# An attention block and a gated MLP in one kernel on one Trainium2 core: a fixed order of scores, maxima and dense products, and weights split by GpSimd

## The chip, the cores and the metric

The kernel runs on one core of a Trainium2 chip, all in float32. The metric is the device time of one execution in microseconds. Three timed runs of the kernel before took 1990.43, 1990.27 and 1982.49 us; the median is 1990.27 us. The profile is of another execution, which took 1979.48 us; its span, from the first to the last instruction, is 1977.7 us.

Five engines work side by side, each through its own queue in order: TensorE (PE: matmuls into PSUM, with weight loads of its own, PEld), VectorE (DVE), ScalarE (ACT), GpSimd (POOL) and SyncE (SP, which here issues nearly all transfers).

## The reference

`x` is 2048 x 512. The result is `x + A(xn) + B(xn)`, where `xn` is the layer norm of `x`:

```python
def _A_ref(x, wqkv, wo):                       # H = 32 heads of 16
    qkv = transpose((x @ wqkv).reshape(B, S, 3, H, Dh), 2, 0, 3, 1, 4)
    q, k, v = qkv[0], qkv[1], qkv[2]
    scores = jnp.einsum("bhqd,bhkd->bhqk", q, k) * (Dh ** -0.5)
    p = _softmax(scores, axis=-1)
    o = jnp.einsum("bhqk,bhkd->bhqd", p, v)
    return transpose(o, 0, 2, 1, 3).reshape(B, S, D) @ wo

def _B_ref(x, w_in, w_sp, b_sp, w_out):        # Fh = 896
    z = _gelu(jnp.einsum("bsd,df->bsf", x, w_in))
    z1 = z[..., :Fh]
    z2 = _layernorm(z[..., Fh:], axis=-1)
    g = jnp.einsum("ts,bsf->btf", w_sp, z2) + b_sp[None, :, None]
    return jnp.einsum("bsf,fd->bsd", z1 * g, w_out)
```

## The kernel before, in words

**Precision.** Nearly all matmul operands are float32r pairs: a value is split into a high part (a copy rounded to float32r) and a low part (the value minus its high part). A product is three matmuls, high x high, low x high and high x low. A weight comes from memory as a raw float32 tile, and `weight()` makes its two parts: the high one on ScalarE or on GpSimd, whichever has less planned work at that point, the low one on GpSimd.

**Attention.** There are 16 pairs of heads, 4 groups of 512 queries and 16 tiles of 128 keys, so 1024 score tiles. For each, `scores()` issues two matmuls (one for each head of the pair, in the two halves of TensorE's rows) into one of three PSUM tiles `sl`, and ScalarE writes their exponential into a tile `pf` (line 63). A softmax needs the row's maximum first: `maxima()` issues the transposed score tile, again two matmuls into one of the three `sl`, and VectorE reduces it (line 754). After every 16 maxima `max_fin` turns the maxima into two extra rows of the operand `qst` by way of memory (`mscr`), so that the scores come out with the maximum taken off. `values()` closes a cycle of CYC = 8 score tiles: it multiplies eight `pf` with `vall`, 32 matmuls that add up in one of the three `sl`. 1024 / 8 = 128 cycles. Every fourth pair `norm_out` fetches sums from memory, divides and stores the attention output as high and low parts (`ohl`).

**Dense work.** Beside the attention run all other products, one after the other, as generators in a list `queue`: Q and K of the other heads (`qk_rest`), the second half of `w_in` (`z2_all`), its first half (`z1_all`), the spatial product (`spatial`: four groups of 512 columns, each with 16 tiles `wsp` of weights against tiles `zs` of the normed z2, in seven units; the last unit of a group is "lone"), the MLP's output (`mlp_out`) and the attention's output (`attn_out`). A dense slot is two matmuls in the two halves of the rows, into the two banks of `dps`. GELU, layer norm, splits and stores of this work, called side work here, are generators too; each step names its engine (`"A"` ScalarE, `"D"` VectorE, `"G"` GpSimd, `"T"` a time that only passes, `"C"` a condition).

**The order.** The whole program is written out by a planner at build time, in Python. It holds an estimated time for TensorE (`T["P"]`) and for the other engines, and the loop at the end of `fused_block` chooses the next TensorE slot: a score or a maximum whenever one of three `sl` is free and a bound allows it, chosen by the backlog of ScalarE and VectorE; else a dense slot; else, after 0.7 us of planned idle time, a filler (two matmuls into `dps` whose result isn't used, line 1103). When eight scores are out and their exponentials planned, it issues `values()`. `advance` places side work on an engine as soon as the plan has the engine free. The engines' queues then hold that order for good: an instruction whose input is late holds up all that stand behind it on its engine.

**Memory.** One ring, `big`, has RING = 18 pieces of 4 KB a partition: weights, `zs`, `xnT`, operands of the outputs. A counter, `room`, says how many are free in the plan. Raw weights have a ring of their own of three half pieces (tag `raw`). `load_z` is called for the tile two places ahead when a quarter of a unit is done. Nearly all loads and stores are issued by SP (`move`, line 115), in the order of the plan: a load whose buffer is still in use holds up all later ones.

Two lines carry the old choice and the old high part:

```python
min(pick, key=lambda p: p[0])[1]()                        # a score or a maximum, by backlog
if max(T["A"], clock()) < max(T["G"], clock()): ...       # weight(): high part by ScalarE or GpSimd
```

Of the kernel before, what the change touches and what calls it, by code (L numbers as in the profile page):

```python
# [31 lines left out]
RING = 18  # L32
LEAD = 24
PF = 7
# [11 lines left out]
def fused_block(ctx, tc, x, wqkv, wo, w_in, w_spT, b_sp, w_out, out):  # L46
# [51 lines left out]
    oscr = [dr.tile([P, 2, S], F32, name=f"oscr{g}") for g in range(4)]  # L98
# [47 lines left out]

    room = {"hilo": 3, "ogrp": 1, "raw": 3, "big": RING}

# [74 lines left out]
    def begin(nm, src, n, blocks=1, t=None, early=None):  # L223


        t = piece(nm) if t is None else t
        rw = t512(nm + "r") if early == "t" else big.tile([P, 512], F32, tag="raw", name=nm + "r", bufs=3)
        dst, hi = rw[:, :n], t[:, 0, :n]
        if blocks > 1:
            src = src.rearrange("(c p) f -> p c f", p=P)  # L230
            dst, hi = (v.rearrange("p (c f) -> p c f", c=blocks) for v in (dst, hi))
# [3 lines left out]
        return t, rw, n  # L235

    def end(loaded, early=False):
        t, rw, n = loaded
        if early:
            nc.vector.tensor_sub(t[:, 1, :n], rw[:, :n], t[:, 0, :n].bitcast(F32))  # L240
        else:
            gps(0.6).tensor_copy(t[:, 0, :n], rw[:, :n])
            gps(1.3).tensor_sub(t[:, 1, :n], rw[:, :n], t[:, 0, :n].bitcast(F32))
        return t

    def prepare(out, loads, freed=None, spare=0):
        for k, *a in loads:
            spawn(weight(out, k, a, freed, spare), 2)

    def weight(out, k, a, freed, spare):  # L250
        yield "C", lambda: room["raw"] > 0 and room["big"] > spare and (freed is None or freed and freed[0] <= clock())
        lease("raw", -1)
        if freed:
            freed.pop(0)
        t, rw, n = begin(*a)
        yield "T", LOAD
        if max(T["A"], clock()) < max(T["G"], clock()):
            yield "A", ta(n)
            act(t[:, 0, :n], rw[:, :n], AF.Copy)
        else:  # L260
            yield "G", 0.61
            nc.gpsimd.tensor_copy(t[:, 0, :n], rw[:, :n])
        yield "G", 0.0026 * n
        nc.gpsimd.tensor_sub(t[:, 1, :n], rw[:, :n], t[:, 0, :n].bitcast(F32))
        lease("raw", 1)
# [137 lines left out]
    def qk_rest():  # L403
        for g in range(NG):
            for m in range(1, 4):
                if m == 3 and g + 1 < NG:
                    fetch_xnT(g + 1, 1)
# [4 lines left out]
                if g == NG - 1 and m == 1:  # L412
                    prepare(w2, [((c, j), f"w2_{c}_{j}", w_in[c * P:(c + 1) * P, FH + j * 448: FH + (j + 1) * 448], 448) for c in range(ND) for j in range(2)], spare=2)
# [27 lines left out]
    def z2_norm(t, z):  # L441

        u = piece(f"z2u{t}").bitcast(F32).rearrange("p a b -> p (a b)")[:, :FH]
# [13 lines left out]
        st = sm.tile([P, 2, 6], F32, tag="zst", name=f"zst{t}", bufs=2)  # L457
        mv = sm.tile([P, 2], F32, tag="zmv", name=f"zmv{t}", bufs=2)
        rs = sm.tile([P, 3], F32, tag="zrs", name=f"zrs{t}", bufs=2)
# [37 lines left out]
    def z2_all():  # L497
        yield from need(lambda: len(w2) == 2 * ND)
        for t in range(NT):
            xt = xts.pop(t)  # L500
            if t + 2 < NT:
                z2_load(t + 2)
            if t == NT - 3:
                prepare(w1, [(f, f"w1_{f}", w_in[:, f * P:(f + 1) * P], D, ND) for f in range(NF)], spare=3)
            if t == NT - 1:
                fetch_xnT(0, 0.5)
            z = piece(f"z2_{t}").bitcast(F32).rearrange("p a b -> p (a b)")[:, :FH]
# [24 lines left out]
    def z1_gelu(f, g, bank, x, u):  # L532
# [13 lines left out]
        after(2.5, lease, "big" if bank else "hilo", 1)  # L546

    def z1_all():
        for g in range(NG):
# [3 lines left out]
            for n, pair in enumerate(pairs):  # L553
                if g == NG - 1 and n == 2:
                    load_b(0)
                    load_z(0)
                    load_z(1)
                    prepare(wsp, [((0, s), *sp_weights(0, s)) for s in range(NT)])
                if n == (2 if g % 2 else 1) and g + 1 < NG:
                    fetch_xnT(g + 1, 1)  # L560
# [28 lines left out]

    def load_z1(g, f):  # L590
# [7 lines left out]
    def spatial():  # L598
        ahead = RING - NT
        for n, (g, (x, y)) in enumerate(units):  # L600
# [7 lines left out]
            freed = []  # L608
            if lone:
                if g + 1 < NG:  # L610
                    prepare(wsp, [((g + 1, s), *sp_weights(g + 1, s)) for s in range(NT)], freed)
                else:
                    prepare(wout, [(f, f"wout{f}", w_out[f * P:(f + 1) * P, :], 512) for f in range(NF)], freed)
# [3 lines left out]
            for s in range(NT):  # L617
                yield from need(lambda: (g, s) in wsp)
# [6 lines left out]
                if lone:  # L625
                    freed.append(clock() + HALF)
                    lease("big", 1)
                    if g + 1 == NG and s == NT - 4:
                        mlp_load(0, 0)
                if s % 4 == 3:  # L630
                    lease("big", 1)
                    if 4 * n + s // 4 + ahead < len(zparts):
                        later(0.7, load_z, 4 * n + s // 4 + ahead)
# [61 lines left out]
    def mlp_out():  # L695
# [13 lines left out]
        for t in range(0, NT, 2):  # L709
            xt = load_x(t)  # L710
            if t == NT - 4:
                selectors()
                prepare(wo_, [(g, f"wo{g}", wo[g * P:(g + 1) * P, :], 512) for g in range(4)])
# [66 lines left out]
    def norm_out(g4, c):  # L780
# [6 lines left out]
        both_ = at_.tile([P, 3, 512], F32, tag="ogrp", name=f"ob{g4}_{c}", bufs=1)  # L787
# [10 lines left out]
        after(5.0, move, both_[rows, 2, :], rscr[g4][c][:nh].rearrange("h (o x) -> h o x", o=1).to_broadcast([nh, DH, 512]))  # L798
# [431 lines left out]
```

## Time and profile before

| | us or share |
|---|---|
| timed runs, median (lowest, highest) | 1990.27 (1982.49, 1990.43) |
| profiled execution: time, span | 1979.48, 1977.7 |
| mean granted TensorE clock | 0.968 |
| GpSimd, VectorE, ScalarE busy, share of the span | 32%, 73%, 64% |
| transfers | 293.55 MB, 148 GB/s |

In the lines that follow, a group or an instruction is given as line of the program, engine, operation, output <- inputs, shapes and count. In a view of stretches each row has the stretch in us from the span's start, its length, the busy time of the engines shown with the number of their instructions, the granted TensorE clock (1.00 is full speed), the share of the DMA engines' time and GB/s. In a view in order of time the first number is the start, the second the duration; brackets hold the engine's idle time just before and what ended it. SPq is SyncE's queue as it issues a transfer. In a list of waits the numbers are the total in us, how often, and the longest.

### The profile page before, as it was taken

Reading aid. Unit: us, or ns where it says so; the run is one execution under the profiler, and the core shown is the slowest. Engines: PE = TensorE matmul, PEld = TensorE weight load, DVE = VectorE, ACT = ScalarE, POOL = GpSimd, SP = SyncE. Lnnn points to the kernel's source line nnn. Section 1 sums busy time; section 2 is a strip of 40 time slices with the busy share of each in tenths; the row PEclk is TensorE's granted clock in tenths of the full one; section 3 lists DMA queues with packets and bytes.
Section 4 is the critical chain, followed back from the end, with each engine's and each line's share of the span. In section 5 each row is a group of like instructions: output and inputs, shape, how many; then the busy total and the mean of one; then the engine's idle time right before and its main releaser. Section 6 shows DMA issues by size and latency. Waiting matters only on the chain. (4 is left out here: it accounts for less than half of the span.)

```text
span 1977.7 us, 37714 instructions
## 1 busy us (share of the span) xinstructions
PE 1866.4 (94%) x14506; PEld 1113.1 (56%) x14506; DVE 1445.2 (73%) x1677; ACT 1257.5 (64%) x1401; POOL 625.5 (32%) x693
## 2 busy tenths in 40 slices
PE   7989999999999999999999899989999999999897
PEld 6755665565565656555655565655655555434552
DVE  5377878888787767776876677757778888767772
ACT  4337778788777756666655566656666666655554
POOL 3222358878988830051014300230023001001100
PEclk9999999999999999999999999999999999878898
DMA  9564653546544554656568564564658755411321
GB/s 325 187 203 162 231 137 103 144 116 156 174 141 149 148 145 120 152 174 146 149 159 214 139 151 126 164 148 129 151 167 197 182 136 150 128 28 56 104 84 64
DMA packets 236588, 293.55 MB, mean 148 GB/s; under 512 B 37352, under 2 KB 137384, under 8 KB 233528
## 3 DMA queue, kind: packets, MB, share of 16 engines
q1 hardware_dynamic: 232184, 281.10, 51.9%
q0 software_dynamic: 4224, 10.04, 1.4%
q8 instruction: 114, 1.87, 0.4%
q14 instruction: 66, 0.54, 0.1%
HBM read 189.08 MB, written 101.98 MB: 147 GB/s over the span
## 5 line engine op out<-in xcount | busy, mean ns | idle before, releaser
L754 DVE TENSOR_REDUCE mm<-sl 128x2 f32<-128x1024 f32 x1024 | 1218.6, 1223 | 273.3 <-PE sl L1046 256.4
L63 ACT ACTIVATE pf<-sl 128x1024 f32<-128x1024 f32 x1024 | 1043.5, 1026 | 488.3 <-PE sl L1032 295.6
L1126 PE MATMUL sl<-pf,vall 128*32 128x512 f32 x4096 | 486.8, 615 | 12.8 <-DVE mm L754 6.0
L1032 PE MATMUL sl<-qst,kst 50*128 50x512 f32 x2048 | 448.8, 425 | 23.0 <-DVE mm L754 12.0
L1046 PE MATMUL sl<-kst,qst 48*128 48x512 f32 x2048 | 447.2, 423 | 21.3 <-ACT pf L63 14.2
L1090 PE MATMUL dps<-wsp,zs 64*128 64x512 f32 x2688 | 441.4, 400 | 20.6 <-DMA zs<-z2scr 18.0
L1090 PEld LDWEIGHTS dps<-wsp,zs 64*128 64x128 f32 x2688 | 276.5, 190 | 74.9 <-DMA zs<-z2scr 24.4
L1032 PEld LDWEIGHTS sl<-qst,kst 50*128 50x128 f32 x2048 | 205.3, 189 | 188.2 <-DVE mm L754 79.5
L1046 PEld LDWEIGHTS sl<-kst,qst 48*128 48x128 f32 x2048 | 202.4, 188 | 174.3 <-ACT pf L63 76.7
L1126 PEld LDWEIGHTS sl<-pf,vall 128*32 128x32 f32 x4096 | 124.8, 112 | 302.4 <-issue 252.8
L1146 DVE TENSOR_TENSOR e<-sl,e 128x512 f32<-128x512 f32 x64 | 44.3, 692 | 167.2 <-PE sl L1126 153.7
L666 POOL TENSOR_TENSOR hhl<-z1i,hhl 128x512 fp32r<-128x512 f32 x28 | 35.6, 1287 | 404.4 <-ACT hhl L63 404.4
L1090 PE MATMUL dps<-w,xt 64*128 64x448 f32 x768 | 111.1, 369 | 1.5
L1090 PE MATMUL dps<-wout,hp 64*128 64x512 f32 x672 | 105.4, 393 | 0.0
L800 POOL TENSOR_TENSOR ob<-ob 128x512 f32<-128x512 f32 (+1 forms) x16 | 20.6, 1285 | 249.8 <-DMA ob<-escr 249.8
L63 ACT ACTIVATE e<-sl 128x512 f32<-128x512 f32 x64 | 38.2, 597 | 75.2 <-PE sl L1126 70.0
L1090 PEld LDWEIGHTS dps<-w,xt 64*128 64x128 f32 x768 | 73.5, 186 | 16.3 <-issue 8.0
L1090 PEld LDWEIGHTS dps<-wout,hp 64*128 64x128 f32 x672 | 64.3, 187 | 10.0
L803 POOL TENSOR_TENSOR ob<-ob 128x512 f32<-128x512 f32 (+1 forms) x16 | 20.6, 1286 | 138.8 <-DMA ob<-rscr 138.8
L399 POOL TENSOR_TENSOR qkhl<-qr,qkhl 128x512 fp32r<-128x512 f32 x24 | 30.5, 1286 | 105.3 <-ACT qkhl L63 105.3
L1090 PE MATMUL dps<-wo,op 64*128 64x512 f32 x288 | 50.8, 429 | 0.9
L484 POOL TENSOR_TENSOR z2hl<-z,z2hl 128x512 fp32r<-128x512 f32 (+1 forms) x32 | 36.8, 1150 | 2.2
(297 smaller groups left out, 1554.0 us busy)
## 6 DMA issues: line engine op xcount, KB each, us to landing
zs<-z2scr SPq DMA_DIRECT2D x192, 256.0 KB
escr<-e SPq DMA_DIRECT2D x60, 256.0 KB
hscr<-hhl SPq DMA_DIRECT2D x28, 512.0 KB
qst<-qscr SPq DMA_DIRECT2D x30, 384.0 KB
kst<-kscr SPq DMA_DIRECT2D x30, 384.0 KB
xscr<-xnT POOLq DMA_DIRECT2D x16, 512.0 KB, 6.1
qscr<-qkhl SPq DMA_DIRECT2D x16, 512.0 KB
kscr<-qkhl SPq DMA_DIRECT2D x16, 512.0 KB
```

What stands on the lines that cost most here:

```text
L63: return nc.scalar.activation(out, in_, func, **kw)
L399: nc.gpsimd.tensor_sub(hl[:, 1, :], raw_, hl[:, 0, :].bitcast(F32))
L484: nc.gpsimd.tensor_sub(hl[:, 1, :w], z[:, lo:lo + w], hl[:, 0, :w].bitcast(F32))
L666: nc.gpsimd.tensor_sub(hl[:, 1, :], z1, hl[:, 0, :].bitcast(F32))
L754: nc.vector.tensor_reduce(mmax[g][:, :, t, kc], sl[k], AX.X, ALU.max)
L800: nc.gpsimd.tensor_add(both_[rows, 0, :], both_[rows, 0, :], both_[rows, 1, :])
L803: nc.gpsimd.tensor_mul(both_[rows, 0, :], both_[rows, 0, :], both_[rows, 2, :])
L1032: nc.tensor.matmul(sl[k][:, j, :], kst[p % 2][rows, kt * P:(kt + 1) * P], qst[p % 2][rows, c * 512:(c + 1) * 512], start=True, stop=True)
L1046: nc.tensor.matmul(sl[k][:, j, :], qst[p % 2][rows, tt * P:(tt + 1) * P], kst[p % 2][rows, kc * 512:(kc + 1) * 512], start=True, stop=True)
L1090: nc.tensor.matmul(dps[:, bank, :w], lhs, rhs, start=go, stop=stop)
L1126: nc.tensor.matmul(sl[k][cols:cols + VW, 0, :], vpack(kt + r, 2 * p + j), pf[:, j * 512:(j + 1) * 512], start=n == n_pv, stop=n == n_pv + ...
L1146: nc.vector.tensor_add(e, sl[k][:, 0, :], e)
```

## The change

Four things change together.

1. The order. A cycle pair has a fixed order, written as two strings of S (scores), M (maxima), D (dense) and V (values). The loop goes through them letter by letter. A letter whose work is used up, or D when the queue has none ready or was run ahead, is passed over. Where an S, M or V can't go yet in the plan, dense slots are taken ahead; where there are none either, a filler comes after 0.15 us of planned idle time (before: 0.7).
2. Side work on ScalarE and VectorE (priority 2) may start in the plan only in the time of a V group, or after it has waited 6 us (`may`, `window`, `AGE`).
3. High parts of weights, and of the attention outputs in `norm_out`, are made by GpSimd alone. Raw weights are pieces of the big ring, up to DEEP = 4 at a time; their own ring goes, RING becomes 19 and `pf` has 8 tiles for 7.
4. Loads: `zs` is loaded by a task of its own (`z_loader`), up to four ahead where there is room; `xnT` is fetched earlier; many leases wait for room before they take a piece; `oscr` is one array, so that the loads of `op` take 64 transfers, not 96.

```diff
-RING = 18
-LEAD = 24
-PF = 7
+RING = 19
+DEEP = 4
+LEAD = 30
+AGE = 6.0
+GATED = "AD"
+ORDER = ('SMDDSDDMDSDDMDDSDMDDSDMDDSDMDDSDMDDSDDMDMV', 'SMDDDDSDMDDSDMDDSDMDDSDMDDDSDMDDSDDDDMSV')
+PF = 8
...
+    window = [-FAR, FAR]
+    def may(k):
+        s0 = max(T[k[0]], k[2])
+        return k[3] < 2 or k[0] not in GATED or window[0] <= s0 <= window[1] or s0 - k[2] > AGE
     def advance(t):
...
-                mine = [k for k in tasks if k[0] == e]
+                mine = [k for k in tasks if k[0] == e and may(k)]
...
+    def weight(out, k, a, spare):
+        yield "C", lambda: raws[0] < DEEP and room["big"] > 1 + spare[0]
+        raws[0] += 1
+        rw = begin(*a)
+        n = rw.shape[1]
         yield "T", LOAD
-        if max(T["A"], clock()) < max(T["G"], clock()):
-            yield "A", ta(n)
-            act(t[:, 0, :n], rw[:, :n], AF.Copy)
-        else:
-            yield "G", 0.61
-            nc.gpsimd.tensor_copy(t[:, 0, :n], rw[:, :n])
+        yield open_("big")
+        t = piece(a[0])
+        yield "G", 0.61
+        nc.gpsimd.tensor_copy(t[:, 0, :n], rw)
         yield "G", 0.0026 * n
...
+    def z_loader():
+        for k in range(len(zparts)):
+            yield "C", lambda: k < zused[0] + 4 and room["big"] > (2 + 2 * (owed[0] > 0) if k > zused[0] + 1 else raws[0] > 0)
+            load_z(k)
...
                 if s % 4 == 3:
-                    lease("big", 1)
-                    if 4 * n + s // 4 + ahead < len(zparts):
-                        later(0.7, load_z, 4 * n + s // 4 + ahead)
+                    zused[0] += 1
+                    later(0.7, lease, "big", 1)
...
-        yield "A", ta(512)
-        act(hl[rows, 0, :], both_[rows, 0, :], AF.Copy)
+        yield "G", 0.61
+        nc.gpsimd.tensor_copy(hl[rows, 0, :], both_[rows, 0, :])
...
-            pick = []
-            if free:
-                if st_ok(t) and kind.count("s") < 2:
-                    pick.append((backlog("A", t), scores))
-                if mx_ok(t) and kind.count("m") < 2 and (n_st - n_pv < CYC or len(free) > 1 or backlog("D", t) < 0.9):
-                    pick.append((backlog("D", t) - 0.2, maxima))
-            if pick:
-                min(pick, key=lambda p: p[0])[1]()
+            op = "V" if n_pv == N else ORDER[line][at_op] if n_st or st_ok(t) else "M"
+            gone = {"S": n_st == N, "M": n_mx == NSTEP, "D": ahead > 0 or not has_dense(t), "V": n_pv == N}[op]
+            if gone and n_st and n_pv < N:
+                ahead -= op == "D" and ahead > 0
+                at_op += 1
+            elif op == "D":
+                dense_slot()
+                at_op += 1
+            elif op == "S" and free and st_ok(t):
+                scores()
+                at_op += 1
+            elif op == "M" and free and (n_st or mx_ok(t)):
+                maxima()
+                at_op += n_st > 0
+            elif op == "V" and 20 <= spent < 27 and has_dense(t):
+                dense_slot()
+            elif op == "V" and free and n_pv + 1 in full:
+                values()
+                at_op, line, ahead, spent = 0, 1 - line, 0, 0
             elif has_dense(t):
                 dense_slot()
-            elif t - active > 0.7 and dfree[0] <= t and not slots and not begun:
+                ahead += n_st > 0
+            elif t - active > 0.15 and dfree[0] <= t and not slots and not begun:
                 filler()
```

More of the change, by code (lines that the diff above doesn't have):

```diff
@@ L546, in z1_gelu @@
         after(2.5, lease, "big" if bank else "hilo", 1)
+        if g == NG - 1 and f == 5:
+            after(2.5, kept.__setitem__, 0, 0)
+    kept = [3]
     def z1_all():
@@ L617, in spatial @@
             for s in range(NT):
-                yield from need(lambda: (g, s) in wsp)
+                yield from need(lambda: (g, s) in wsp and 4 * n + s // 4 in zp)
                 zt, w, c = zp[4 * n + s // 4], wsp[g, s], slice((s % 4) * P, (s % 4 + 1) * P)
@@ L712, in mlp_out @@
                 selectors()
-                prepare(wo_, [(g, f"wo{g}", wo[g * P:(g + 1) * P, :], 512) for g in range(4)])
+                prepare(wo_, [(g, f"wo{g}", wo[g * P:(g + 1) * P, :], 512) for g in range(4)], spare=(-9,))
             for q in range(2):
@@ L936, in fused_block @@
         load_x(2)
-        w0 = [end(l, True) for l in w0]
+        for r, t in zip(w0r, w0):
+            end(r, t, True)
         turn_x(0)
@@ L940, in fused_block @@
         init_rows(0)
-        wv = [end(l, True) for l in wv]
+        for r, t in zip(wvr, wv):
+            end(r, t, True)
         norm = norm_x(1, 2)
@@ L985, in fused_block @@
         active = 0.0
+        line = at_op = ahead = spent = 0
         begun = set()
```

126 lines of the change are left out of this document (64 added, 62 removed).

## The prediction

> **What bounds the kernel now.** I read the shares of the engines first, then the value products (line 1126) cut into stretches at their own starts, then the order of time around the longest stretches.
>
> ```profile
> span 1977.7 us, 37714 instructions
> PE 1866.4 (94%) x14506; PEld 1113.1 (56%) x14506; DVE 1445.2 (73%) x1677; ACT 1257.5 (64%) x1401; POOL 625.5 (32%) x693
> ```
> TensorE is the only engine near full, and its busy time is no slack measure here: it also counts matmuls that run at half clock. The work comes in 128 cycles: in each, one group of value products (32 matmuls, V) closes eight score slots (S, line 1032), about eight slots of maxima (M, line 1046) and, as a rule, 24 dense slots (D, line 1090). The next view counts V's matmuls in each stretch; its count over 32, rounded, is the number of cycles (a few records are missing or fall on an edge).
>
> ```profile
> core 0: us, PE busy (x) PEld busy (x), PEclk, DMA share, GB/s
> 137.90:247.30 109.40, 29.17 (x260) 7.57 (x262) 1.00 0.59 193
> 247.30:478.20 230.90, 58.21 (x512) 15.16 (x512) 1.00 0.45 126
> 478.20:525.90 47.70, 12.55 (x100) 3.13 (x102) 0.96 0.75 201
> 525.90:706.60 180.70, 47.59 (x416) 12.57 (x416) 1.00 0.49 147
> 706.60:725.60 19.00, 3.66 (x35) 0.96 (x35) 0.91 0.57 131
> ...
> 874.90:908.40 33.50, 8.98 (x67) 2.24 (x67) 0.95 0.61 161
> ...
> 1061.80:1121.60 59.80, 12.84 (x100) 2.99 (x102) 0.89 0.72 191
> 1121.60:1284.70 163.10, 43.65 (x384) 11.48 (x384) 1.00 0.53 140
> 1284.70:1324.50 39.80, 7.28 (x64) 1.94 (x64) 0.91 0.80 174
> ...
> 1475.50:1506.60 31.10, 7.31 (x68) 1.94 (x69) 1.00 0.76 212
> 1506.60:1703.70 197.10, 54.67 (x483) 14.22 (x483) 1.00 0.63 160
> 1703.70:1793.40 89.70, 29.82 (x192) 6.76 (x192) 0.74 0.22 56
> 1793.40:1923.90 130.50, 31.61 (x256) 8.01 (x256) 0.92 0.30 89
> 1923.90:1977.70 53.80, 19.36 (x128) 4.54 (x128) 0.83 0.16 60
> ```
> An undisturbed cycle is that of 1121.6 to 1284.7: 163.1 / 12 = 13.59 us, at clock 1.00. The chain of what ended last has the last V's start:
>
> ```profile
> 1960.56 4.49 PE sl L1126 x32
> ```
> So 17.1 us lie behind it, and the 127 cycles from 137.9 to it have a mean of 14.35 us: 0.76 us a cycle, 97 us in all, are lost somewhere. Where: in short stretches with much DMA and a clock below 1.00 (from 478, 707, 875, 1062, 1285 and 1475 us), in the stretch at clock 0.74, in the eight cycles after it (130.5 / 8 = 16.3), and evenly in 247 to 478 (230.9 / 16 = 14.43). One of the short ones, opened:
>
> ```profile
> 1061.18 0.67 SPq L115 DMA_DIRECT2D wsp_0r<-in_w_spT  x1
> ...
> 1066.52 0.61 POOL L262 CAST wsp<-wsp_0r 128x512 fp32r<-128x512 f32 x1 [12.45 <-DMA wsp_0r<-in_w_spT]
> 1067.05 0.63 ACT L63 ACTIVATE wsp<-wsp_1r 128x512 fp32r<-128x512 f32 x1 [5.83 <-DMA wsp_1r<-in_w_spT]
> ...
> 1067.59 1.01 ACT L63 ACTIVATE pf<-sl 128x1024 f32<-128x1024 f32 x1
> ...
> 1068.64 1.92 PE L1126 MATMUL sl<-pf,vall 128*32 128x512 f32 x4 [3.24 <-ACT pf L63]
> ...
> 1071.38 0.39 SPq L115 DMA_DIRECT2D zs<-z2scr  x1
> ```
> A raw weight takes 1066.52 - 1061.18 = 5.3 us to land. ScalarE, which works in the order of its queue, stood 5.83 us at the high part of a weight; the exponentials stood behind it, and TensorE stood behind them. The load of zs waits in SP's queue behind raw weights, and TensorE then waits for it too:
>
> ```profile
> PEld dps L1090 <- DMA zs<-z2scr: 24.4, 22, 3.2
> ...
> PE dps L1090 <- DMA zs<-z2scr: 18.0, 16, 2.8
> ```
>
> **The change, part by part.** The order of the changed program's instructions shows the same numbers of S, M, D and V in the same 128 cycles; it has 135 filler slots in place of 39. A slot's price is (1019.70 - 1019.23) / 2 = 0.235 us:
>
> ```profile
> 1019.23 0.63 PE L1090 MATMUL dps<-wsp,zs 64*128 64x512 f32 x4
> 1019.70 0.40 PE L1032 MATMUL sl<-qst,kst 50*128 50x512 f32 x2
> ```
> The fixed order gives an ordinary pair of cycles 48 or 49 D, 16 S, 16 M and two V; the old order has the same numbers there. I take nothing from the order itself in such cycles: 13.59 stays.
>
> *High parts to GpSimd, loads earlier.* 63 ScalarE copies (47 of weights, 16 of attention outputs) become 63 GpSimd casts, 63 x 0.61 = 38 us more on an engine busy 625.5 us; no ScalarE instruction waits for a raw weight any more. Now GpSimd does: behind a late raw weight on its queue stand the subtractions for h and for the attention output, whose readers on TensorE come 60 slots later or more. Without that cover the 47 weights would put 47 x 0.61 = 29 us ahead of D. In the order of both programs I count TensorE's work between the instruction that releases a zs load (through SP's queue) and the first use: as a rule some 38 slots' worth (9 us) before, 58 (13.5 us) after. The exception is one load in each of the three later column groups, which stands behind the last raw weight: 22 slots, 5.2 us, against the 5.3 us landing above. The six short stretches hold 3+1+2+3+2+2 = 13 cycles and 230.9 us; 13 x 13.59 = 176.7, so 54.2 us are at stake. At most all of it goes; at least ScalarE's share, the 3.24 us of V plus a like clock loss at each of some four places, about 20. I keep three late loads at 3.5 us, between nothing and the 19.0 - 13.59 = 5.4 of the stretch from 706.6: **-44**. SP is relieved a little: 32 DMAs of op fewer.
>
> *First group of spatial weights.* In cycles 42 to 44 the new order has only 15, 0 and 12 D, and no filler, because an accumulation stands open in the dense banks. Priced like the cycles without D (89.7 / 6 = 14.95): 3 x 1.36 = **+4**.
>
> *The stretch without D.* Before, cycles 111 to 116 have no D at all and three fillers. VectorE paces them, TensorE idles in small pieces, and its clock falls, so V itself grows:
>
> ```profile
> 1731.95 6.14 PE L1126 MATMUL sl<-pf,vall 128*32 128x512 f32 x32
> ...
> 1740.98 0.51 PE L1032 MATMUL sl<-qst,kst 50*128 50x512 f32 x2 [0.39 <-DVE mm L754]
> ...
> 1890.34 3.64 PE L1126 MATMUL sl<-pf,vall 128*32 128x512 f32 x32
> ```
> After, the dense work ends later: two such cycles are left there (115 and 116), with 23 fillers. V then costs 3.64, not 6.14, and the six go to 13.59: 89.7 - 81.5 = **-8**; nothing, if the clock falls all the same. The 96 added fillers, 96 x 0.235 = 22.6 us, stand mostly in cycles with few or no D (50 of all fillers in cycles 17 to 27), where TensorE would be idle: I price them at 0, with 22.6 as the other end.
>
> By the Trainium skill, "TensorE: Matmul & The Clock Gate", section "Part 1: The HAM clock gate", the clock halves only after an idle window of about 3.4 us. This trace doesn't agree: in 1703.7 to 1793.4 the granted clock is 0.74, and the waits shown there are like the 0.39 us above. By the rule, fillers would buy nothing here.
>
> *Attention out.* The same queueing on ScalarE, later:
>
> ```profile
> 1894.61 1.28 POOL L803 TENSOR_TENSOR ob<-ob 96x512 f32<-96x512 f32 x1 [12.62 <-DMA ob<-rscr]
> ...
> 1895.92 0.63 ACT L63 ACTIVATE ohl<-ob 96x512 fp32r<-96x512 f32 x1 [3.41 <-POOL ob L803]
> ...
> 1898.00 0.79 PE L1032 MATMUL sl<-qst,kst 50*128 50x512 f32 x2 [2.43 <-ACT pf L63]
> ```
> The copy that blocked is a GpSimd cast now, and the new order leaves 60 slots or more from release to the first product with ohl, where it left 36. 130.5 - 8 x 13.59 = 21.8 us at stake, nothing to all; I keep 2 of it: **-20**.
>
> *Side work beside V.* Side work of ScalarE and VectorE may start in V's time only, or once it has waited 6 us. In 247 to 478, the stage with most side work, cycles take 14.43 and not 13.59: 16 x 0.84 = 13.4; from 525.9 to 706.6 (180.7 / 13 = 13.90) it is 13 x 0.31 = 4. The loss may double as well if the work overruns V. I take half of each as gained: **-9**. The stage's end has 72 D too few in cycles 23 to 28; fewer D don't lengthen a cycle with fillers, and the D come back in 111 to 114.
>
> *Start.* 28 more slots stand ahead of the first V (+6.6), and a wait goes, because xnT is fetched some 130 slots earlier:
>
> ```profile
> 122.83 1.65 PE L1090 MATMUL dps<-xnT__1126,wqk 64*128 64x512 f32 x6 [4.64 <-DMA xnT__1126<-xscr]
> ```
> Together **+2**. The end (53.8 us) I leave: cycle 125 gains 24 D (5.6 us) and the fillers save about as much clock.
>
> Sum: -44 + 4 - 8 - 20 - 9 + 2 = -75; 1977.7 - 75 = 1902.7 us of span. The profiled execution took 1979.48, 1.8 more than its span, and the three runs 1982.49, 1990.27 and 1990.43, up to 10.8 more than it. I add 1.8 and 5.5: **1910**.
>
> **Rivals.** *All stalls go*, side work costs nothing, no late zs: 1977.7 - 54.2 - 8 - 21.8 - 13.4 - 4 + 2 = 1878, so 1885. For it: all slacks counted above grew. Against it: the three loads with 5.2 us.
>
> *Only the ScalarE blocks go; the loads stay late*, because raw weights now fill whole pieces of the ring (19 in place of 18, and three half pieces fewer). Then 20 of the 54 and none of the 9: 1910 + 24 + 9 = 1943.
>
> *Side work overruns V.* VectorE needs nearly all of the time outside V for eight maxima, 8 x 1.223 = 9.8 of 13.59 - 3.64 = 9.95 us:
>
> ```profile
> L754 DVE TENSOR_REDUCE mm<-sl 128x2 f32<-128x1024 f32 x1024 | 1218.6, 1223 | 273.3 <-PE sl L1046 256.4
> ```
> Work that starts at V's end delays the first M and, in a fixed order, everything behind it: TensorE can't take D first, as it did. Place: every cycle. Price: the 14.43 us of 247 to 478, or more with wider D. With 137.9 + 2 ahead and 17.1 behind, a mean cycle of 14.7 gives 2024, run 2031; it decides for slower from (2000.2 - 7.3 - 157) / 127 = 14.46 us. Against it: outside that stage cycles keep 13.6 with the same M.
>
> *Fillers are pure cost and the clock isn't held*: 1910 + 22.6 + 8 = 1941. The 0.74 beside idle times of under half a microsecond speaks against it. It is what the rule of the Trainium skill quoted above would give.
>
> **Chances.** Forecast 0.45, all stalls gone 0.20, loads late 0.15, fillers 0.05, overrun 0.12, and 0.03 for gains that cancel near the old time. The median of the runs can tell about 0.5%, 10 us. Faster 0.82, within it 0.05, slower 0.13, a little of each case moved for what I don't see. The forecast's own range is 1885 to 1935; for eight in ten it takes in the first rival and the two at 1941 to 1943, and stops short of the overrun: 1868 to 1978.
>
> **What would show it.** Right: no ScalarE wait for a DMA or for ob; cycles of 13.6 through the former short stretches; clock 0.95 or more in cycles 115 and 116; waits for zs of a few us in cycles 58, 72 and 86 only. Wrong: ordinary cycles over 14 us, V waiting for pf, GpSimd casts late so that dps products wait for wsp, or a clock still near 0.74 beside the fillers.

## The result and the profile after

| | before | after |
|---|---|---|
| timed runs, median of 4 (lowest to highest), us | 1988.37 (1982.49 to 1990.43) | 1926.74 (1920.97 to 1928.88) |
| ratio, 95% interval | 1 | 0.969 [0.966, 0.972] |
| profiled execution: time, span, us | 1979.48, 1977.7 | 1920.97, 1919.2 |

The change saves 62 us by the medians and 58.5 us of span. The page of the changed kernel, engines and granted clock in 40 slices (nine tenths or more is a 9):

```profile
PE 1842.2 (96%) x14698; PEld 1109.2 (58%) x14698; DVE 1440.6 (75%) x1677; ACT 1224.5 (64%) x1338; POOL 657.9 (34%) x756
...
PEclk9999999999999998999999999999999999999999
```

GpSimd has the 63 copies of ScalarE (693 instructions before, 756 now, 32 us more), and TensorE has no long slow stretch any more. The V matmuls of the changed kernel, cut at the same cycles as the stretches of before (stretch, length, busy time of PE and PEld with counts, clock, share of the DMA engines, GB/s):

```profile
core 0: us, PE busy (x) PEld busy (x), PEclk, DMA share, GB/s
...
244.80:468.60 223.80, 58.26 (x512) 15.04 (x512) 1.00 0.43 114
468.60:509.50 40.90, 10.92 (x96) 2.80 (x96) 1.00 0.60 172
...
689.50:702.20 12.70, 3.63 (x32) 0.93 (x32) 1.00 0.79 172
...
854.80:881.50 26.70, 7.25 (x64) 1.85 (x64) 1.00 0.32 91
881.50:1048.20 166.70, 40.04 (x352) 10.31 (x352) 0.97 0.71 168
1048.20:1094.60 46.40, 10.95 (x100) 2.83 (x100) 0.96 0.59 154
...
1261.10:1287.90 26.80, 7.28 (x68) 1.88 (x71) 1.00 0.57 132
...
1470.30:1676.30 206.00, 54.59 (x480) 14.05 (x480) 0.99 0.60 153
1676.30:1755.30 79.00, 21.85 (x192) 5.63 (x192) 1.00 0.59 158
1755.30:1868.80 113.50, 29.15 (x260) 7.51 (x260) 1.00 0.35 102
```

Row against row, three things are to be seen. The six short stretches shrink from 230.9 to 184.7 us (five of them here; the sixth, 31.1, stays). Their neighbours grow: 881.5 to 1048.2 takes 166.7 where the same 11 cycles took 153.4 (1061.8 - 908.4), and 1470.3 to 1676.3 takes 206.0, not 197.1. And the six cycles that had no D before (after the change only the last two of them, 115 and 116, have none) go from 89.7 us at clock 0.74 to 79.0 at 1.00, the attention's output from 130.5 to 113.5.

TensorE's waits for zs are a little rarer and no shorter in total. The lists of waits (total, times, longest), after:

```profile
PEld dps L1122 <- DMA zs<-z2scr: 27.0, 19, 3.3
PE dps L1122 <- DMA zs<-z2scr: 22.6, 16, 3.0
```

Before, these were 24.4 us (22 times) and 18.0 (16 times). They stand in other cycles now: 57, 58, 62, 65, 66, 72, 86, 94 and 98, each of them 15 to 21 us long where an undisturbed one takes 13.4.

### The profile page after: what moved, and what is told of

Read it like the earlier page. It is cut to its first block, busy times and chain, and to the rows that moved or that the text cites. A ratio compares the mean times of both kernels' runs of the same rounds, so it can differ in the third digit from the quotient of the medians.

```text
span 1919.2 us, 38036 instructions
## 1 busy us (share of the span) xinstructions
PE 1842.2 (96%) x14698; PEld 1109.2 (58%) x14698; DVE 1440.6 (75%) x1677; ACT 1224.5 (64%) x1338; POOL 657.9 (34%) x756
## 4 chain that ended last, share of the span: by engine, by line
PE 77%; DMA 7%; DVE 6%; POOL 5%; issue 2%; ACT 2%; SPq 1%; DVEq 0%; ACTq 0%; POOLq 0%
PE dps L1122 29%; PE sl L1160 20%; PE sl L1064 12%; PE sl L1078 11%; DVE mm L780 4%; DMA zs<-z2scr 3%; SPq L119 1%; POOL wsp L278 1%; ACT pf L67 1%; PE dps L1136 1%; PE sl L230 1%; PE sl L231 1%; PE sl L232 1%; POOL wsp L276 1%; DMA wsp_8r<-in_w_spT 1%
## 5 line engine op out<-in xcount | busy, mean ns | idle before, releaser
L1122 PE MATMUL dps<-wsp,zs 64*128 64x512 f32 x2688 | 458.5, 399 | 24.5 <-DMA zs<-z2scr 22.6
L1160 PE MATMUL sl<-pf,vall 128*32 128x512 f32 x4096 | 470.9, 600 | 0.2
L1078 PE MATMUL sl<-kst,qst 48*128 48x512 f32 x2048 | 436.5, 412 | 10.6 <-ACT pf L67 5.3
L1064 PEld LDWEIGHTS sl<-qst,kst 50*128 50x128 f32 x2048 | 201.1, 186 | 231.6 <-issue 90.0
L1160 PEld LDWEIGHTS sl<-pf,vall 128*32 128x32 f32 x4096 | 120.8, 110 | 272.8 <-issue 242.6
L1122 PE MATMUL dps<-wout,hp 64*128 64x512 f32 x672 | 110.7, 392 | 0.0
L829 POOL TENSOR_TENSOR ob<-ob 128x512 f32<-128x512 f32 (+1 forms) x16 | 20.6, 1285 | 146.5 <-DMA ob<-rscr 146.5
L415 POOL TENSOR_TENSOR qkhl<-qr,qkhl 128x512 fp32r<-128x512 f32 x24 | 30.3, 1282 | 87.4 <-ACT qkhl L67 75.3
L1136 PE MATMUL dps<-brow,onesr 64*128 64x512 f32 x270 | 47.6, 400 | 1.3 <-DVE z L452 0.4
L1122 PE MATMUL dps<-wo,op 64*128 64x512 f32 x288 | 46.2, 396 | 0.9 <-DVE fin L871 0.4
```

The lines of the kernel that those rows point to most:

```text
L415: nc.gpsimd.tensor_sub(hl[:, 1, :], raw_, hl[:, 0, :].bitcast(F32))
L829: nc.gpsimd.tensor_mul(both_[rows, 0, :], both_[rows, 0, :], both_[rows, 1, :])
L1064: nc.tensor.matmul(sl[k][:, j, :], kst[p % 2][rows, kt * P:(kt + 1) * P], qst[p % 2][rows, c * 512:(c + 1) * 512], start=True, stop=True)
L1078: nc.tensor.matmul(sl[k][:, j, :], qst[p % 2][rows, tt * P:(tt + 1) * P], kst[p % 2][rows, kc * 512:(kc + 1) * 512], start=True, stop=True)
L1122: nc.tensor.matmul(dps[:, bank, :w], lhs, rhs, start=go, stop=stop)
L1136: nc.tensor.matmul(dps[:, bank, :], onesr[r:r + 64], brow[r:r + 64], start=True, stop=True)
```

## The experiments

All ratios are to the kernel before on the same chip, with a 95% interval. Times by cycle are worked out from the starts of V in each trace; cycle n runs from V group n to the next. Four groups of cycles are used throughout: *z stages* (8 to 22 and 30 to 39), *former stalls* (52 to 54, 65 to 68 and 80 to 82), *behind them* (55 to 58, 69 to 72 and 83 to 86), and *tail* (111 to 124). Each row is one profiled execution, and these lie off the median of their kernel's runs by up to 8.9 us (the kernel before 8.9 below and the changed one 5.8, e4 6.0 above and e12 7.6), so a few us say little. The kernel before, timed again beside each batch of runs, had medians from 1983 to 1988 us; between batches the ratios are the better measure.

| us | z stages | former stalls | behind them | 94 and 98 | 111 to 116 | 117 to 124 | span |
|---|---|---|---|---|---|---|---|
| before | 355.8 | 176.5 | 162.1 | 28.0 | 89.7 | 130.5 | 1977.7 |
| after | 347.0 | 142.6 | 183.0 | 37.2 | 79.0 | 113.4 | 1919.2 |
| before + fillers (e8) | 357.0 | 179.5 | 161.6 | 26.1 | 78.0 | 121.5 | 1951.3 |
| before + fillers + gate (e13) | 345.2 | 144.9 | 194.2 | 28.0 | 87.4 | 116.5 | 1973.1 |
| before + high parts (e6) | 359.4 | 164.3 | 163.7 | 32.9 | 99.7 | 127.7 | 1999.9 |
| after without gate (e2) | 365.6 | 170.6 | 161.0 | 29.0 | 78.1 | 114.0 | 1926.2 |
| after + late rows (e1) | 346.4 | 143.9 | 177.2 | 38.9 | 78.6 | 113.5 | 1910.1 |
| after, old choice, late rows (e11) | 350.0 | 139.3 | 170.8 | 26.5 | 79.0 | 113.9 | 1896.0 |

### Fillers: taken out of the new kernel, and put into the old one

e3 plans the fillers and doesn't issue them; their results are not used by anything.

```diff
-            for r, bank in ((0, 0), (64, 1)):
-                nc.tensor.matmul(dps[:, bank, :], onesr[r:r + 64], brow[r:r + 64], start=True, stop=True)
             T["P"] += SLOT
```

> The plan and the order are those of the changed kernel, but the 135 fillers are not issued; they compute nothing that is used. Theory (fillers hold the clock): V groups take 4 to 6 us in cycles 115, 116, 123 and 126 to 128 and in 23 to 27, the granted clock falls below 0.85 there, and the time is 1940 to 1950 us. Rival (a clock that falls only after an idle time of some 3.4 us, by the Trainium skill, TensorE: Matmul & The Clock Gate, Part 1): fillers cost up to 135 x 0.235 = 32 us and hold nothing, 1895 to 1925 us.

Measured: 1947.67 us, 0.981 [0.978, 0.985], in the theory's range: 21 us slower than the changed kernel, at a mean granted clock of 0.966 where that had 0.989. e8 is the kernel before with one number changed.

```diff
-            elif t - active > 0.7 ...
+            elif t - active > 0.15 ...
```

> The kernel before with one number changed: fillers after 0.15 us of planned idle time, not 0.7. Theory: the clock of 0.74 in the six cycles without dense work and of 0.83 at the end goes to 0.95 or more, V there takes 3.6 us, and 12 to 22 us are gained: 1962 to 1972 us. Rival: the fillers' own time eats the gain, or an open accumulation forbids them there: 1980 to 1990 us.

Measured: 1953.71 us, 0.985 [0.983, 0.988], 29 us faster than the kernel before on the same chip (1983.03), and more than the theory's 12 to 22. TensorE in cycles 111 to 116 of e8 (columns as above, without PEld):

```profile
1702.20:1780.20 78.00, 75.42 (x522) 1.00 0.25 64
```

The same six cycles without D take 78.0 at clock 1.00, where they took 89.7 at 0.74: 11.7 us, and the eight after them 9. So the fillers are the largest single part that could be isolated, and they are no cost. The changed kernel's own cycles 115 and 116, in order of time, show what they do:

```profile
1741.97 3.64 PE L1160 MATMUL sl<-pf,vall 128*32 128x512 f32 x32
...
1746.12 0.40 PE L1136 MATMUL dps<-brow,onesr 64*128 64x512 f32 x2
1746.50 0.50 PE L1064 MATMUL sl<-qst,kst 50*128 50x512 f32 x2
```

Fillers stand between the scores and maxima, where TensorE idled for a few tenths of a microsecond before, and V takes 3.64 us, not 6.14. How short those pieces were, TensorE's waits in 1703.7 to 1793.4 us of the kernel before show; this is the largest group, and no other has a longer wait:

```profile
PE sl L1032 <- DVE mm L754: 6.4, 19, 0.5
```

### High parts by GpSimd: alone in the old kernel, and undone in the new one

e6 is the kernel before with the two edits of `weight()` and `norm_out` alone; e4 is the changed kernel with ScalarE's share given back.

```diff
e6, in the kernel before:
-        if max(T["A"], clock()) < max(T["G"], clock()):
-            yield "A", ta(n)
-            act(t[:, 0, :n], rw[:, :n], AF.Copy)
-        else:
-            yield "G", 0.61
-            nc.gpsimd.tensor_copy(t[:, 0, :n], rw[:, :n])
+        yield "G", 0.61
+        nc.gpsimd.tensor_copy(t[:, 0, :n], rw[:, :n])
...
-        act(hl[rows, 0, :], both_[rows, 0, :], AF.Copy)
+        nc.gpsimd.tensor_copy(hl[rows, 0, :], both_[rows, 0, :])
e4, in the changed kernel: the same two edits the other way
```

> The kernel before with one part of the change alone: high parts of weights and of the attention outputs by GpSimd. The prediction's theory (ScalarE's blocks cost 20 us where raw weights load and most of 21.8 us in attention out): 1945 to 1965 us against 1984 before. Rival, after the run that put the high parts back in the changed kernel and moved it by 2 us: TensorE waits for the same late loads by another way, 1975 to 1990 us.

> The high parts of weights go to ScalarE or GpSimd by the plan's choice again, and those of the attention outputs to ScalarE, as before the change; the rest is the changed kernel. Theory: ScalarE stands at late inputs again with the exponentials behind it: 17 us in attention out and 10 to 20 us where raw weights load, 1945 to 1965 us. Rival: the loads are early enough in the new plan, or ScalarE does the copies beside V: 1920 to 1932 us.

Measured: e6 2003.97 us, 1.0115 [1.008, 1.015], slower than theory and rival both said; e4 1929.15 us, 0.9725 [0.970, 0.975], as the rival said. In the old plan the high parts on GpSimd do shorten the former stalls (176.5 to 164.3 us), and more is lost in cycles 95 to 116; in e6 cycles 99 to 110 and 111 to 116 read:

```profile
1543.70:1716.70 173.00, 164.38 (x1278) 0.96 0.52 134
1716.70:1816.40 99.70, 91.21 (x454) 0.73 0.21 48
```

against 158.4 and 89.7 us in the kernel before; why the first of them grew isn't settled. In the new plan it makes no difference that 4 runs can tell who makes them, though ScalarE's blocks do come back in e4 (waits, total, times, longest):

```profile
ACT wsp L67 <- POOL wsp L282: 14.1, 8, 4.1
...
ACT wsp L67 <- DMA wsp_2r<-in_w_spT: 8.7, 3, 5.8
```

ScalarE's waits for raw weights and for GpSimd are back, and the total stays. Whether these waits lie off the path that sets the end isn't shown: e4 also loads the raw weights a cycle later and is slower in some cycles (3 us in the z stages, 4 in the former stalls) and faster in others (8 behind them, 10 in cycles 94 and 98).

### The fixed order

e5 is the changed kernel with the old choice of the next slot by backlog.

```diff
-            op = "V" if n_pv == N else ORDER[line][at_op] if n_st or st_ok(t) else "M"
...
+            if pick:
+                min(pick, key=lambda p: p[0])[1]()
+            elif has_dense(t):
+                dense_slot()
```

with the old bounds (`LEAD` 24, scores and maxima limited by the V group, the old `hold`) and two conditions for room changed, one made stricter and one looser.

> The changed kernel with the old choice of slots (score or maximum by backlog, old bounds and LEAD 24) in place of the fixed order; fillers after 0.15 us, loads, side work beside V and GpSimd high parts stay as changed, but for two conditions on free pieces of the ring (w1 may load with 3 pieces spare, xnT waits for 2 more) without which the plan doesn't come to an end. Theory: in ordinary cycles the fixed order is worth 13.59 - 13.42 us, some 17 us over the stages with dense work, so 1935 to 1950 us. Rival: the order is worth nothing, the gain came with fillers and loads, 1918 to 1932 us.

Measured: 1926.82 us, 0.972 [0.969, 0.974], the same as the changed kernel's 1926.74, and the rival's forecast. The order of the slots by itself is worth nothing that these runs can tell, to within some 7 us.

### The gate on side work: undone in the new kernel, alone in the old one

e2 is the changed kernel with `GATED = ""`. e13 is e8 with the gate added:

```diff
+    window = [-FAR, FAR]
...
+    def may(k):
+        s0 = max(T[k[0]], k[2])
+        return k[3] < 2 or k[0] not in "AD" or window[0] <= s0 <= window[1] or s0 - k[2] > 6.0
...
-                mine = [k for k in tasks if k[0] == e]
+                mine = [k for k in tasks if k[0] == e and may(k)]
...
+            window[:] = T["P"], T["P"] + CYC / 2 * ROUND
```

> GATED is empty: side work of ScalarE and VectorE starts as soon as the plan has the engine free, as before the change; the rest is the changed kernel. Theory: the gate gives the fall from 14.43 to 14.09 us a cycle in the z2 stage and from 13.90 to 13.6 in the z1 stage, some 9 us: 1933 to 1940 us. Rival: the fixed order gives that by itself, then 1922 to 1930.

> The kernel before with fillers after 0.15 us (e8) and with the rule that side work of ScalarE and VectorE starts in the time of V only, or after 6 us. Theory (the gate is worth its time by itself): cycles 8 to 22 go from 217.2 us to 211 to 213 and 30 to 39 from 139.8 to about 136, and the median from 1953.7 to 1941 to 1947. Rival (the gate only works in the fixed order, where TensorE can't take dense slots first): both groups stay within 1.5 us and the median is 1950 to 1958.

Measured: e2 1927.45 us, 0.971 [0.969, 0.973]; e13 1975.13 us, 0.994 [0.992, 0.997]. Both medians miss their theory. Without the gate the new kernel is as fast as with it (the rival of e2, though not for its reason: the z stages do lose), and in the old one (1953.71 with fillers alone) the gate costs some 20 us, more than either side of e13 allowed, though it shortens the z stages as its theory said (357.0 to 345.2). That is not because the gate does nothing. TensorE in the new kernel without the gate, cycles 8 to 22, then 52 to 54, 55 to 58, 65 to 68, 69 to 72, 80 to 82 and 83 to 86:

```profile
core 0: us, PE busy (x), PEclk, DMA share, GB/s
230.50:455.70 225.20, 214.80 (x1787) 1.00 0.45 120
858.20:904.60 46.40, 43.08 (x346) 0.96 0.74 210
904.60:958.20 53.60, 53.46 (x452) 1.00 0.61 147
1039.10:1109.60 70.50, 60.75 (x453) 0.88 0.77 208
1109.60:1163.30 53.70, 53.56 (x455) 1.00 0.53 126
1257.30:1311.00 53.70, 45.58 (x342) 0.90 0.83 209
1311.00:1364.70 53.70, 53.56 (x452) 1.00 0.43 119
```

and the same cycles of the changed kernel, with the gate:

```profile
230.30:441.70 211.40, 205.87 (x1724) 1.00 0.42 111
841.10:881.50 40.40, 40.26 (x340) 1.00 0.39 106
881.50:948.40 66.90, 58.90 (x453) 0.95 0.83 203
1032.90:1094.60 61.70, 56.83 (x456) 0.97 0.66 160
1094.60:1153.30 58.70, 55.90 (x453) 0.97 0.75 201
1247.30:1287.90 40.60, 40.46 (x344) 1.00 0.66 145
1287.90:1345.20 57.30, 54.84 (x456) 1.00 0.69 199
```

In the z stage the gate saves 14 us, as a stage that is full of side work would. In the spatial product it moves the stalls: the busy transfers and the lost time go from the former stalls to the cycles behind them. What moves is the raw weights. Their loads, counted by the cycle in which SyncE issues them:

| group of columns | second | third | fourth |
|---|---|---|---|
| before, and e8 | 51 to 53 | 65 to 68 | 79 to 81 |
| after without gate (e2) | 51 to 54 | 65 to 68 | 79 to 81 |
| after | 55 to 57 | 69 to 72 | 83 to 85 |
| before + fillers + gate (e13) | 54 to 57 | 68 to 71 | 82 to 85 |

In both programs the gate shifts the 16 raw weights of a group by three to four cycles, nearer to their use. This is shown both ways: taking the gate out of the new kernel brings the old cycles and the old stalls back (142.6 to 170.6 us), putting it into the old one removes them (179.5 to 144.9). In e13 all of that is paid again behind them (161.6 to 194.2 us) and more in cycles 99 to 116 (236.5 to 254.1); in the new kernel 22 of the 28 us are, and 8 more in cycles 94 and 98. That the gate does this by keeping pieces of the ring longer is only argued.

### Loads of zs four ahead

```diff
-            yield "C", lambda: k < zused[0] + 4 and ...
+            yield "C", lambda: k < zused[0] + 2 and ...
```

> The changed kernel with zs loaded at most two ahead (in place of four), as the kernel before did. Theory (earlier zs loads are what shortened the former short stretches): before to after, cycles 52 to 54 went from 48.3 to 40.4 us, 65 to 68 from 74.0 to 61.7 and 80 to 82 from 54.2 to 40.5, 33.9 us together; half or more of that comes back, TensorE's waits for zs grow by as much, and the median is 1944 to 1961. Rival (what shortened them is that raw weights no longer stand in ScalarE's way, or that the plan has more room): these cycles stay within 6 us of the changed kernel's 142.6 and the median is 1920 to 1934.

Measured: 1928.38 us, 0.971 [0.968, 0.975], as the rival said; the former stalls take 142.1 us, the changed kernel's 142.6. Loading zs up to four ahead, rather than two, buys nothing.

### What makes zs late: SyncE's queue, in part

The changed kernel's zs load before cycle 62, in SyncE's queue (start, time to issue):

```profile
975.52 0.42 SPq L119 DMA_DIRECT2D mscr<-ms  x1
978.13 0.55 SPq L119 DMA_DIRECT2D hscr<-hhl  x1
978.73 1.77 SPq L119 DMA_DIRECT2D z1i<-z1scr  x2
980.60 2.73 SPq L119 DMA_DIRECT2D qst<-mscr  x4
...
987.14 2.59 SPq L119 DMA_DIRECT2D zs<-z2scr  x4
```

and TensorE at its first use:

```profile
993.89 0.49 PE L1122 MATMUL dps<-wsp,zs 64*128 64x512 f32 x1 [1.17 <-DMA zs<-z2scr]
```

If the piece of that zs was free when TensorE's run of products before it ended, at 974.8 us (the trace doesn't name the pieces), the load was issued 12 us later, behind a row of transfers. Among them is the load of the maxima's rows, `qst<-mscr`, which can't go until the store `mscr<-ms` ahead of it has landed in memory. Here that wait cost nothing: from 978.1 on SyncE issues one transfer after the other, 9 us of them, 2.7 for these four rows, and before that it stood 2.1 us for GpSimd's h. Elsewhere it does stand. SyncE's waits for that store, in the whole of the changed kernel:

```profile
SPq L119 <- DMA mscr<-ms: 82.6, 36, 8.4
```

e1 tells the plan that this round trip takes longer, for all groups but the first, so that the load stands further back in the queue:

```diff
-after(3.3, move, qst[p % 2] ...
+after(9.0 if g else 3.3, move, qst[p % 2] ...
-maxready[g] = ends[0] + 8.5
+maxready[g] = ends[0] + (13.5 if g else 8.5)
```

> The loads of the maxima's rows into qst are put 9.0 us behind max_fin in the plan, not 3.3, and the scores that need them 5 us later; everything else is that of the changed kernel. Theory: the zs loads that are late in cycles 57, 58, 62, 65, 66, 72, 86, 94 and 98 (45 us over 13.42 a cycle) are late because SyncE's queue stands at these four small loads until mscr has landed; then most of it goes, 1890 to 1905 us, and the wait of SP for mscr falls from 82.6 us to under 30. Rival: the transfers themselves are slow (bandwidth); then zs is as late as before and the time is 1920 to 1930.

Measured: 1912.91 us, 0.963 [0.961, 0.966], 14 us faster than the changed kernel by the medians, 11 by the ratios, 9 in span; this lies between theory and rival. SyncE's waits in e1, and then TensorE's:

```profile
SPq L119 <- DMA mscr<-ms: 33.5, 14, 6.1
```

```profile
PEld dps L1122 <- DMA zs<-z2scr: 16.7, 12, 4.7
...
PE dps L1122 <- DMA zs<-z2scr: 12.1, 10, 4.4
```

SyncE waits 49 us less for this store and TensorE 21 us less for zs, in its two lists. SyncE does not wait less in all: its waits add up to 1131 us in the changed kernel and 1126 in e1; it stands at other transfers instead. Where the theory holds can be seen in cycle 57, by SyncE's waits from 920 to 931 us of the changed kernel and, below, from 917 to 927 us of e1:

```profile
SPq L119 <- DMA mscr<-ms: 3.8, 1, 3.8
...
SPq L119 <- DMA mscr<-ms: 0.6, 1, 0.6
```

The pair of zs loads behind it goes at 930.7 us in the changed kernel and at 926.8 in e1, and cycle 58 takes 15.0 us, not 18.8 (cycle 57 itself stays, 20.9 for 21.3). A transfer in line behind another's round trip was part of what made zs late.

The rival has its part too. On the chain that ended last in the changed kernel stand two loads of zs that took about twice as long from issue to landing as the one at 987.79 (7.1 us):

```profile
909.98 13.44 DMA zs<-z2scr
...
1028.46 15.11 DMA zs<-z2scr
```

In e1 a raw weight of 9.2 us stands on the chain in place of the first, in cycle 57. The second, for cycle 65, is there again, with 14.3 us, and in e11 with 16.0; cycles 65 and 66, in which the DMA engines are 0.87 busy, take 34.8 us in the changed kernel and 35.6 in e1. So loads that are slow after their issue remain, and e1 doesn't touch those; what slows them wasn't tried.

e9 goes further: e1, and the stores of `hscr` and `oscr` issued by GpSimd.

```diff
-store(hscr[g][:, :, :, f, :], ...)
+nc.gpsimd.dma_start(raw(hscr[g][:, :, :, f, :]), ...)
-store(oscr[:, :, g4, c * 512:(c + 1) * 512], hl)
+nc.gpsimd.dma_start(raw(oscr[:, :, g4, c * 512:(c + 1) * 512]), raw(hl))
```

> The run with the maxima's rows fetched later, and with the 40 stores of h and of the attention output issued by GpSimd, which makes their data, in place of SyncE, which waits for GpSimd before them. Theory: zs loads in cycles 58, 62, 66 and 94 no longer stand behind those waits, 1898 to 1908 us against 1913. Rival: those loads are late by transfers already under way, or the issue costs GpSimd more than it saves: 1909 to 1920 us.

Measured: 1917.8 us, 0.968 [0.964, 0.971]. No gain on e1 can be seen, as the rival said; if anything it is a little slower.

e12 is e8 with the edit of e1, in the old kernel.

> The kernel before with two numbers changed: fillers after 0.15 us (e8) and the late loads of the maxima's rows (e1). Theory (SyncE's queue standing at a load whose data are still on their way to memory and back delays all transfers behind it, in the old order as in the new: its wait for the maxima's store was 82.9 us there): the 1953.7 of e8 falls by 8 to 18, to 1936 to 1946. Rival (in the old order zs is late because its piece comes free late, not because of SyncE's queue): 1949 to 1957.

Measured: 1945.09 us, 0.979 [0.976, 0.983], against 0.985 [0.983, 0.988] for e8. The time is in the theory's range, and the gain is 9 us by the medians, 13 by the ratios. The trace can't say where it comes from: the profiled execution was the slowest of the four, and its span, 1950.9, is that of e8, 1951.3. In it TensorE's waits for zs fall only from 22.0 and 20.9 to 19.3 and 18.7 us.

### The best version: old choice with late rows

e11 is e5 with the edit of e1.

> The changed kernel with the old rule for choosing slots (e5) and with the late loads of the maxima's rows (e1). Theory (the two are independent: e5 was worth nothing, e1 14 us): 1906 to 1918. Rival (the late rows only fitted the fixed order, and the old rule puts a maximum where its row would now be late): 1920 to 1935, with score slots waiting for qst.

Measured: 1897.94 us (1895.13 to 1900.57), 0.955 [0.952, 0.958]: the fastest of all, 29 us below the changed kernel and faster than either theory said. TensorE's two waits for zs fall to 11.1 and 6.9 us. TensorE in cycles 57 and 58 (34.0 us) and in cycle 98 (13.0 us):

```profile
907.00:941.00 34.00, 29.89 (x228) 0.95 0.92 223
...
1477.70:1490.70 13.00, 13.00 (x110) 1.00 0.91 269
```

Of the changed kernel's stalled cycles 57, 58, 72, 86, 94 and 98 only the first two are long still (34.0 us for 40.1). Against e1, the start is 5.6 us earlier (first V at 130.2, not 135.8), cycles 57, 58, 72, 86, 94 and 98 are 20.6 us shorter (88.4 for 109.0), and cycles 30 to 45 are 9.6 longer (226.7 for 217.1). The two parts are not independent: the old choice is worth nothing where rows are early and 15 us where they are late.

## Why the prediction came out as it did

The forecast was 1910, the result 1926.74: inside the range, and in the forecast's own (1885 to 1935), 17 us too low. That it came so near is in part luck: the largest term was twice too large, and the reasons given for the two largest, -44 and -20, did not hold in the runs. The sum against what the same cycles show, in span:

| step | predicted | measured |
|---|---|---|
| high parts to GpSimd, loads earlier: short stretches and the cycles between them | -44 | -46.2 + 25.8 = -20.4 |
| first group of spatial weights (cycles 42 to 52) | +4 | +3.3 |
| stretch without D | -8 | -10.7 |
| attention out | -20 | -17.0 |
| side work beside V (137.9 to 478, 525.9 to 706.6) | -9 | -8.3 |
| start | +2 | -2.0 |
| end | 0 | -3.4 |
| sum | -75 | -58.5 |

The 7.3 us added from the span to the median were right: 1926.74 - 1919.2 = 7.5. (In their working the runs lie up to 10.95 us above the profiled execution, 1990.43 - 1979.48, not 10.8.)

**Late loads: the step that failed.** "I keep three late loads at 3.5 us" was the wrong term. The three loads foreseen, in cycles 58, 72 and 86, were late indeed, and six more cycles with them; the short stretches gave the -46.2, but the cycles between them took 13.3 + 3.4 + 0.2 + 8.9 = 25.8 back. Slots from release to first use (13.5 us) were the wrong test: a load may be released early and still be issued late, as the 12 us of cycle 62, because SyncE's queue stands or is busy with other transfers, and it may land late: two took 13.4 and 15.1 us, where the prediction reckoned with the 5.3 of a raw weight. The prediction gave no time to SyncE's own waits and issues. The rival "only the ScalarE blocks go; the loads stay late" had this term's size, 20 of the 54, though not its cause, and it was wrong on the side work. The cause that the prediction named for the gain fell as well: moving ScalarE's high parts alone takes 12 us off the former stalls and loses more elsewhere (e6), and giving them back costs nothing that the runs can tell (e4). What emptied cycles 52 to 54, 65 to 68 and 80 to 82 is the gate (e2, e13), which the prediction priced for the z stages only: it moved the raw weights, and most of the gain there was paid back behind them.

**Stretch without D, and the fillers.** Right in direction and place: V at 3.64, clock 1.00. Part of it is the D that come back in 111 to 114, but e8, with no D there, has 78.0 us at 1.00 as well. What fillers do in the whole kernel is more than this term: alone in the old kernel they gave 29 us. The price of nothing for the 96 added fillers held; the rival "fillers are pure cost", 1941, falls by e3 and e8. By the Trainium skill, "TensorE: Matmul & The Clock Gate", section "Part 1: The HAM clock gate", they would have bought nothing; the runs disagree. In 1703.7 to 1793.4 us of the kernel before, at a granted clock of 0.74, TensorE has no wait longer than 0.5 us. The same page of the Trainium skill, section "A second HAM failure mode: psum-queue depth-cycling", reports a kernel whose clock oscillated through frequent short idle pieces between groups of matmuls. That agrees with the 0.74 of before and the 1.00 of e8.

**Attention out.** The size was right (-17 for -20), the reason not: e8 alone takes 9 of it, and e4, with ScalarE's copies back, keeps all (110.6 us in cycles 117 to 124). The other 8 are neither the gate's nor the order's (without them the new kernel has 114.0 in e2 and 113.8 in e5); they come from something in the new plan that was not isolated.

**Side work.** The half taken as gained in the z stages was right; without the gate the new kernel's cycles 8 to 22 take 225.2 us, 15.0 a cycle, more than the kernel before took. The rival "side work overruns V" did not occur: cycles 8 to 22 of the changed kernel take 211.3 / 15 = 14.1 us, less than before (216.1 / 15 = 14.4).

**Start.** The +2 was -2. The wait for xnT went as foreseen (no wait of a dense product for it is left in the list); where the rest was saved wasn't followed.

**Order.** "I take nothing from the order itself" was right (e5), as long as the rows are loaded early; where they are loaded late it costs 15 us (e1 and e11).

What stays open: of the 62 us, fillers alone give 29 in the old kernel. Order, high parts, gate and the four-ahead loads are each worth nothing, to within some 7 us, when undone in the new kernel, yet the old kernel with fillers and gate takes 50.8 and 49.9 us for cycles 69 to 71 and 83 to 85, in which the new one loads the same raw weights in 40.0 each. What was not tried alone is raw weights as pieces of the big ring with the waits for room, the 19th piece and the eighth `pf`, the earlier `xnT` and the single `oscr`. Which of them it is, or whether it takes several at once, stays open.

## What to carry to other kernels

When a stall disappears from one place, add up the cycles behind it before counting a gain: a change of a plan's timing moves transfers, and 26 of 46 us came back here. Look at what the transfer queue itself waits for: a load that depends on a store's round trip, issued too early, holds up every free load behind it, and moving it back by 5.7 us in the plan was worth 9 to 14 us. Parts that are worth nothing one at a time can be worth something together (the old choice with late rows, 15 us), so take the best version from runs of pairs.

## What the runs showed of the hardware

TensorE's clock fell to 0.74 over 90 us with no wait longer than 0.5 us, and fillers of 0.235 us a slot held it at 1.00 in the same cycles: 78.0 us for 89.7. Issuing a transfer is not free for SyncE: a load of zs, or of the maxima's rows, takes it 0.6 to 0.7 us in these rows of e1, so a pair takes 1.27. The second pair below shows 2.77 because the row takes in a wait between its two loads; the last line is SyncE's waits from 982.45 to 985.3 us:

```profile
978.41 1.27 SPq L119 DMA_DIRECT2D zs<-z2scr  x2
979.72 2.68 SPq L119 DMA_DIRECT2D qst<-mscr  x4
982.49 2.77 SPq L119 DMA_DIRECT2D zs<-z2scr  x2
...
SPq L119 <- DMA ob<-escr: 1.5, 1, 1.5
```

The rows show e1's edit as well: here a pair of zs loads goes ahead of `qst<-mscr`, where the changed kernel had them all behind it.
